# Regrouping one attention group's vector work in a two-layer attention and MLP kernel: heads gathered by DMA, layernorm statistics on ScalarE, two products and a softmax moved behind an output projection, V computed before Q and K

## The chip, the cores and the metric

The kernel runs on one core of a Trainium2 chip. The metric is the device time of one execution in microseconds (us). Before the change it is 1232.96 us, the median of 3 runs (1232.81 to 1233.49). Names of engines: PE is TensorE (PEld its weight loads), DVE is VectorE, ACT is ScalarE, POOL is GpSimd, SP is SyncE. The profiled span is about 2 us shorter than the device time, because it begins at the first instruction and ends at the last.

## The reference

Two layers, each a local dilated attention block and an MLP, with a layernorm ahead of each and a residual after each. The sequence has 2048 rows of 1024; 32 heads of 32; each position attends to 8 positions, two apart.

```python
def _A_ref(x, wqkv, wo):                      # H = 32, Dh = 32, W = 8, dil = 2
    qkv = (x @ wqkv).reshape(B, S, 3, H, Dh)  # -> q, k, v
    idx = pos[:, None] - off[None, :]         # off = arange(8) * 2, masked where negative
    kg, vg = k[:, :, idx_c, :], v[:, :, idx_c, :]
    logits = einsum("bhsd,bhswd->bhsw", q, kg) * scale
    attn = softmax(where(mask, logits, -1e9))
    o = einsum("bhsw,bhswd->bhsd", attn, vg)
    return o.reshape(B, S, D) @ wo
def _B_ref(x, w1, b1, w2, b2):                # F = 3584
    return gelu(x @ w1 + b1) @ w2 + b2
# ... cut: setup
x = x + _A_ref(_layernorm(x), A_wqkv, A_wo)
x = x + _B_ref(_layernorm(x), B_w1, B_b1, B_w2, B_b2)
# ... the same two lines again, same weights
```

## The kernel before

The rows are cut into 4 groups of 512 for each layer; groups are numbered n = 0 to 7 over both layers. PE works through the stages QKV(n), WO(n) (output projection), FFN1(n), FFN2(n) in an order fixed by the program. While PE is in one stage, DVE computes the attention of a later group: eight products q*k for the logits, with a tree of adds (`new_prod`), the softmax (`attend`), the spread of its weights over partitions (`spread`, by DMA), and eight weighted sums of values (`av`). A list of "sides" says after which step of the PE stage each piece is recorded: `at(5, attend, 1)` records the softmax of group 1 after step 5, and `each(av, 1, 10, 2, 0, 4)` records the weighted sums 0 to 3 of group 1 from step 10 on, two steps apart. A scheduler then turns this into one fixed order for each engine, when the program is built; the engine keeps to that order. `hold` forbids that later DVE pieces move ahead of earlier ones.

There are six PSUM accumulators (`acc`); a matmul into a new one waits until an older one has been read out (evicted), and in the FFN2 stage DVE evicts. And qT and kT have one buffer each at this point, so Q of group 3 can't be written before the products of group 2 have read theirs.

```python
def acc_tile():
    return psum.tile([P, T], F32, name="acc", bufs=6)

def head_sum(n, last=True):                  # sum over the 4 partitions of a head, on PE
    # ... cut: L, prod
    for wh in range(2):
        for tb in range(NTT):
            mm(L[tb * H:(tb + 1) * H, wh * 4:(wh + 1) * 4, :], lhsT=smat[:],
               rhs=prod[:, tb, wh * 4:(wh + 1) * 4, :], start=start,
               stop=last, skip_group_check=True, tile_position=(0, tb * H))

def gather(n):                               # the same sum prepared by DMA, added on DVE
    prod = s["prods"].pop(0)
    Lq = bigp.tile([P, HP, W, P], BF16, name="big")
    for j in range(HP):
        pool.dma_start(Lq[:, j, :, :], prod[j::HP, :, :, :])

def attend(n):
    if "Lq" in s:
        # e = Lq[0] + Lq[1], then + Lq[2], + Lq[3]   (DVE)
    else:
        head_sum(n)
    # ... cut: mask, maximum, subtract
    act.on = 1 < n < N - 1                   # the exponential keeps its place in ACT's order
    act.activation(e[:], e[:], ACT.Exp, scale=SCALE)
    # ... cut: sum, reciprocal, multiply -> a

# FFN2, after the last quarter of the contraction, for each of the four row tiles:
    vec.tensor_tensor(out=tmp[:], in0=ps, in1=b2bc[:, out_cols], op=ALU.add)   # the eviction
    vec.tensor_tensor(out=xs, in0=tmp[:], in1=xs, op=ALU.add)

# the stages around the change:
    stage(gen_ffn1(0), sides=at(5, attend, 1) + at(5, spread, 1) + at(5, hold) + each(new_prod, 2, 2, 1)
          + at(10, gather, 2) + at(10, hold) + each(av, 1, 10, 2, 0, 4))
    stage(gen_ffn2(0), sides=at(0, ln_stats_ahead, 3) + at(15, hold) + at(15, ln_a, 3, None, True)
          + each(av, 1, 16, 1, 4, 8) + at(23, hold))
    for n in range(1, N - 2):
        stage(gen_wo(n), sides=at(0, spread, n + 1) if n > 1 else at(7, hold) + at(7, attend, 2))
        stage(gen_qkv(n + 2), sides=(at(0, spread, 2) if n == 1 else []) + each(av, n + 1, 0, 2, 0, 3))
        # ... cut
        gather(n + 2)
        stage(gen_ffn1(n), sides=... + each(av, n + 1, 8, 2, 3, 8))
        if n + 3 < N:
            stage(gen_ffn2(n), sides=at(0, hold) + at(0, attend, n + 2) + at(2, ln_a, n + 3))
```

## Time and profile before

The page's line of busy times (engine, busy us, share of the span, count of instructions) and its chain that ended last (shares of the span by engine and line, where L118 is the helper that issues all matmuls), kernel before:

```profile
PE 1222.2 (99%) x5739; PEld 632.6 (51%) x5789; DVE 861.9 (70%) x922; ACT 307.3 (25%) x491; POOL 87.2 (7%) x207
PE acc L118 98%; DMA wt<-in_A_wqkv_dram 1%; SPq L93 0%; PE L L118 0%; PE L L219 0%; DVE x L93 0%
```

The view of waits of PE alone (who waited for whom: total us, times, longest), kernel before:

```profile
PE acc L219 <- DVE xn L93: 1.5, 1, 1.5
PE acc L118 <- DVE big L93: 1.1, 1, 1.1
PE acc L118 <- DMA wt<-in_A_wqkv_dram: 0.3, 1, 0.3
```

All three waits lie in the first 12.1 us. After that PE never waits. The Trainium skill, "Perfetto Trace Analysis", warns at its top that matmul busy time misjudges the distance to the roofline, because matmuls are pipelined. Here the busy share isn't used for that; what counts is that no other engine ever makes PE wait, so only fewer PE cycles can help, and any new wait costs time.

The cost of one head sum is read from the chain in order of time (start us, duration us, what), kernel before:

```profile
149.78 10.14 PE acc L118 x47
159.93 0.55 PE L L118 x8
160.47 38.31 PE acc L118 x177
```

The eight matmuls of group 1 hold PE for 0.55 us.

Now DVE around FFN2(1), from its timeline (start us, us, engine, line, operation, output<-inputs, count, and in brackets the idle time before it with what ended it), kernel before:

```profile
265.15 1.22 DVE L93 TENSOR_TENSOR e<-big 128x1024 f32<-128x1024 bf16 x1
...
276.26 0.69 DVE L93 TENSOR_TENSOR tmp<-e 128x512 f32<-128x512 f32 x1 [2.47 <-ACT e L93]
...
285.79 4.50 DVE L93 TENSOR_TENSOR big<-abc,vT 128x4096 bf16<-128x4096 bf16 x2 [5.81 <-DMA abc<-a]
...
296.55 2.28 DVE L93 TENSOR_TENSOR big<-qT,kT 128x4096 bf16<-128x4096 bf16 x1
...
371.65 0.69 DVE L93 TENSOR_TENSOR tmp<-acc,b2bc 128x512 f32<-128x512 f32 x1
```

The softmax of group 2 begins at 265.2 (`e<-big`, the first add of its gathered logits; `tmp<-e` at 276.3 is the first step after its exponential). Values of group 2 (`big<-abc,vT`) begin at 285.8, products of group 3 (`big<-qT,kT`) at 296.6, and the first eviction of FFN2(1) (`tmp<-acc,b2bc`) starts at 371.65. PE has no wait there: its timeline shows FFN2(1) as one piece.

```profile
350.35 48.51 PE L118 MATMUL acc<-wt,hT 128*128 128x512 bf16 x219
```

| kernel before | us | view |
|---|---|---|
| device time | 1232.96 | times |
| PE waits after 12.1 us | 0 | waits of PE |
| one head sum on PE | 0.55 | chain in order of time |
| one product or its add | 2.3 | groups (2286 ns; 2291 ns for an add) |
| first eviction of FFN2(1) starts | 371.65 | timeline of DVE |
| FFN2(1) starts / WO(2) starts on PE | 350.35 / 398.70 | timeline of PE |

### The profile page before, as it was taken

What the parts mean: (1) busy time and instruction counts of PE and PEld (TensorE: products, weight loads), DVE (VectorE), ACT (ScalarE), POOL (GpSimd) and SP (SyncE); (2) the same over time, 40 slices, a digit from 0 to 9 for tenths busy, and PEclk for the clock granted to TensorE, in tenths of its full rate; (3) what the DMA queues carried; (4) which work ended last, traced back from release to release, by engine and by line L of the source; (5) the groups of instructions that cost most, each with busy time, mean ns of one, the idle gap of its engine ahead of it and who ended that gap; (6) DMA issues with size and microseconds to landing.
All of it is one profiled execution on the core that took longest, in us unless ns stands there. A gap on an engine that the chain in (4) does not pass through costs nothing.

```text
span 1230.8 us, 13962 instructions
## 1 busy us (share of the span) xinstructions
PE 1222.2 (99%) x5739; PEld 632.6 (51%) x5789; DVE 861.9 (70%) x922; ACT 307.3 (25%) x491; POOL 87.2 (7%) x207
## 2 busy tenths in 40 slices
PE   9999999999999999999999999999999999999998
PEld 7666544456444564445544465444654444444444
DVE  7989899988998599375993759937599797011001
ACT  4343152014320143202431024310244101400310
POOL 3010010010010000100011000010000002000000
PEclk9999999999999999999999999999999999999999
DMA  9954665656556654856447565486664558446441
GB/s 290 300 179 143 182 222 185 201 154 209 181 165 215 180 162 163 229 172 186 150 163 238 171 171 170 158 223 202 171 196 145 188 196 208 151 158 196 155 135 52
DMA packets 219391, 225.06 MB, mean 183 GB/s; under 512 B 68194, under 2 KB 187136, under 8 KB 217024
## 3 DMA queue, kind: packets, MB, share of 16 engines
q1 hardware_dynamic: 214704, 208.69, 55.5%
q0 software_dynamic: 4624, 15.49, 3.3%
q8 instruction: 45, 0.74, 0.2%
q14 instruction: 18, 0.15, 0.0%
HBM read 191.11 MB, written 4.72 MB: 159 GB/s over the span
## 4 chain that ended last, share of the span: by engine, by line
PE 99%; DMA 1%; issue 0%; SPq 0%; DVE 0%
PE acc L118 98%; DMA wt<-in_A_wqkv_dram 1%; SPq L93 0%; PE L L118 0%; PE L L219 0%; DVE x L93 0%
## 5 line engine op out<-in xcount | busy, mean ns | idle before, releaser
L118 PE MATMUL acc<-xnT,wt 128*128 128x512 bf16 (+1 forms) x3392 | 720.9, 375 | 0.4 <-DMA wt<-in_A_wqkv_dram 0.3
L118 PEld LDWEIGHTS <-wt 128*128 128x128 bf16 x3392 | 400.5, 119 | 319.1 <-issue 1.4
L118 PE MATMUL acc<-wt,hT 128*128 128x512 bf16 (+1 forms) x1780 | 386.0, 376 | 2.1
L118 PEld LDWEIGHTS <-hT 128*128 128x128 bf16 x1820 | 178.1, 98 | 208.9
L93 DVE TENSOR_TENSOR big<-big 128x1024 bf16<-128x1024 bf16 (+2 forms) x184 | 245.2, 1360 | 2.2
L93 ACT ACTIVATE hT<-acc,b1T 128x512 bf16<-128x512 f32 x224 | 152.7, 688 | 332.3 <-PE acc L118 332.1
L93 DVE TENSOR_TENSOR big<-qT,kT 128x4096 bf16<-128x4096 bf16 x64 | 143.8, 2286 | 48.4 <-ACT kT L93 47.8
L93 DVE TENSOR_TENSOR big<-abc,vT 128x4096 bf16<-128x4096 bf16 x64 | 144.7, 2286 | 14.0 <-DMA abc<-a 13.4
L93 DVE TENSOR_TENSOR tmp<-acc,b2bc 128x512 f32<-128x512 f32 x56 | 38.6, 690 | 146.7 <-PE acc L118 143.7
L93 ACT CAST qT<-acc 128x512 bf16<-128x512 f32 (+1 forms) x72 | 38.0, 545 | 351.1 <-PE acc L118 351.1
L118 PE MATMUL acc<-wt,oT 128*128 128x512 bf16 x440 | 97.4, 379 | 0.4
L93 DVE BATCH_NORM_STATS2 stats<-x 128x6 f32<-128x512 bf16 x128 | 85.6, 682 | 4.5 <-DMA x<-in_A_x_dram 3.4
L118 PEld LDWEIGHTS <-oT 128*128 128x128 bf16 x448 | 43.8, 98 | 52.8
L93 DVE TENSOR_TENSOR x<-acc,big 128x512 bf16<-128x512 f32 (+1 forms) x9 | 5.7, 633 | 90.0 <-PE acc L118 90.0
L93 ACT CAST vT<-acc 128x512 bf16<-128x512 f32 x64 | 37.5, 586 | 83.3 <-PE acc L118 83.3
L93 ACT CAST kT<-acc 128x512 bf16<-128x512 f32 x64 | 37.4, 587 | 67.0 <-PE acc L118 67.0
L93 POOL TENSOR_TENSOR rstd<-mv,eps_t 128x1 f32<-128x1 f32 x56 | 14.2, 253 | 515.4 <-DVE mv L93 509.4
L93 DVE TENSOR_TENSOR x<-acc,x 128x512 bf16<-128x512 f32 x64 | 42.9, 671 | 4.8 <-PE acc L118 4.4
L93 DVE TENSOR_SCALAR xn<-x,mv,rstd 128x1024 bf16<-128x1024 bf16 x52 | 28.4, 547 | 20.2 <-POOL rstd L93 20.1
L93 DVE TENSOR_TENSOR x<-tmp,x 128x512 bf16<-128x512 f32 x56 | 38.7, 690 | 1.3
L93 POOL DMA_DIRECT2D big<-big x24 | 13.3, 565 | 256.3 <-DVE big L93 237.6
L93 POOL TENSOR_TENSOR rstd<-rstd,mhalf 128x1 f32<-128x1 f32 x56 | 31.0, 553 | 4.4
(68 smaller groups left out, 228.8 us busy)
## 6 DMA issues: line engine op xcount, KB each, us to landing
wt<-in_B_w_dram SPq DMA_DIRECT2D x56, 1024.0 KB, 5.7
wt<-in_B_w_dram SPq DMA_DIRECT2D x64, 896.0 KB, 4.9
wt<-in_A_wqkv_dram SPq DMA_DIRECT2D x46, 1024.0 KB, 5.6
wt<-in_A_wo_dram SPq DMA_DIRECT2D x16, 1024.0 KB, 5.0
big<-big POOLq DMA_DIRECT2D x24, 256.0 KB, 3.6
abc<-a POOLq DMA_DIRECT2D x24, 256.0 KB, 5.3
x<-in_A_x_dram SPq DMA_DIRECT2D x16, 256.0 KB, 6.2
out_dram<-x SPq DMA_DIRECT2D x31, 128.0 KB, 2.1
```

The costliest lines, as they stand in the source:

```text
L93: inst = f(*args, **kwargs)
L118: return pe(nc.tensor.matmul(*args, **kwargs))
```

## The change

The intent is to take the head sum of group 1 off PE (a DMA gather and three DVE adds replace it). DVE is full in that stretch, so room is made: the fourth layernorm's statistics go to ScalarE, and the last two products and the softmax of group 2 go behind WO(1). As these then still need group 2's Q and K when QKV(3) begins, V of group 3 is computed first. The diff, cut to its core:

```diff
     def ln_stats_ahead(g):
+        junk = lnp.tile([P, D], BF16, name="xn", bufs=3)
         for tt in range(NTT):
-            ln_stats(g * NTT + tt, mv_ahead[:, tt, :], rstd_ahead[:, tt, :])
+            # ... cut: t, mean, var, less
+            act.activation(junk[:], x[t][:], ACT.Identity, scale=-1.0 / D, accum_out=less[:])
+            act.activation(junk[:], x[t][:], ACT.Square, bias=less[:], accum_out=var)
+            pool.tensor_scalar(out=mean, in0=less[:], scalar1=-1.0, scalar2=None, op0=ALU.mult)
+            # ... cut: two POOL operations for rstd
 def gen_qkv(...)
+        if v_first:
+            wv = load_qkv(2)          # then V, before Q and K
 def gather(n)
-        Lq = bigp.tile([P, HP, W, P], BF16, name="big")
+        Lq = attp.tile([P, HP, W, P], BF16, name="abc") if n == 1 else bigp.tile([P, HP, W, P], BF16, name="big")
-    def attend(n):
+    def logits(n):                    # up to the subtraction of the maximum
+    def weights(n):                   # exponential, sum, division
-        if n < 2:                     # max by one reduce; spread through DRAM
+        if n == 0:
         stage(q2, sides=each(new_prod, 1, 0, 1, 5, 8))
+        gather(1)
-    stage(gen_ffn1(0), sides=at(5, attend, 1) + at(5, spread, 1) + at(5, hold) + each(new_prod, 2, 2, 1)
-          + at(10, gather, 2) + at(10, hold) + each(av, 1, 10, 2, 0, 4))
+    stage(gen_ffn1(0), sides=each(new_prod, 2, 2, 1, 0, 3) + at(5, hold) + at(5, attend, 1) + at(5, spread, 1) + at(5, hold) + each(new_prod, 2, 6, 1, 3, 6)
+           + at(10, hold) + each(av, 1, 10, 2, 0, 4))
-        stage(gen_wo(n), sides=at(0, spread, n + 1) if n > 1 else at(7, hold) + at(7, attend, 2))
-        stage(gen_qkv(n + 2), sides=(at(0, spread, 2) if n == 1 else []) + each(av, n + 1, 0, 2, 0, 3))
+        stage(gen_wo(n), sides=at(0, spread, n + 1) if n > 1 else at(7, hold))
+        stage(gen_qkv(n + 2, v_first=n == 1), sides=each(av, n + 1, 0, 2, 0, 3) if n > 1 else
+              each(new_prod, 2, 0, 1, 6, 8) + at(1, gather, 2) + at(6, hold) + at(6, logits, 2) + at(15, weights, 2) + at(15, spread, 2) + each(av, 2, 16, 3, 0, 3))
```

More of the change, by code (lines that the diff above doesn't have):

```diff
@@ L205, in ln_stats_ahead @@
     def ln_stats_ahead(g):
+        junk = lnp.tile([P, D], BF16, name="xn", bufs=3)
         for tt in range(NTT):
-            ln_stats(g * NTT + tt, mv_ahead[:, tt, :], rstd_ahead[:, tt, :])
+            t, mean, var = g * NTT + tt, mv_ahead[:, tt, 0:1], mv_ahead[:, tt, 1:2]
+            less = lnp.tile([P, 1], F32, name="less")
+            act.activation(junk[:], x[t][:], ACT.Identity, scale=-1.0 / D, accum_out=less[:])
+            act.activation(junk[:], x[t][:], ACT.Square, bias=less[:], accum_out=var)
+            pool.tensor_scalar(out=mean, in0=less[:], scalar1=-1.0, scalar2=None, op0=ALU.mult)
+            rstd = rstd_ahead[:, tt, :]
+            pool.tensor_scalar(out=rstd, in0=var, scalar1=1.0 / D, scalar2=EPS, op0=ALU.mult, op1=ALU.add)
+            pool.tensor_tensor(out=rstd, in0=rstd, in1=mhalf[:], op=ALU.pow)
     def ln_norm(t, mv, rstd, xn=None):
@@ L318, in new_prod, with gen_qkv @@
                 vec.tensor_tensor(out=tree[-1][:], in0=tree[-1][:], in1=b[:], op=ALU.add)
-    def gen_qkv(n, parts=1, defer=False, qk_pool=None, v_late=False, qk_next=None):
+    def gen_qkv(n, parts=1, defer=False, qk_pool=None, v_late=False, qk_next=None, v_first=False):
         g = n % NG
@@ L326, in gen_qkv, with values @@
         qk_pool = qk_pool or attp
+        if v_first:
+            wv = load_qkv(2)
         wq = wq_first if n == 0 else load_qkv(0)
-        wk = load_qkv(1)
+        if not v_first:
+            wk = load_qkv(1)
+        def values():
+            vT = attp.tile([P, NCH, HALO + T], BF16, name="vT", bufs=2)
+            s["vT"] = vT
+            act.on = n > 2
+            act.copy(vT[:, :, 0:HALO], (zhalo if g == 0 else vhalo)[:])
+            act.on = False
+            for c in range(NCH):
+                ps = qkv_chunk(wv, c, xnT)
+                act.copy(vT[:, c, HALO:], ps[:])
+                yield
+            if g + 1 < NG:
+                act.copy(vhalo[:], vT[:, :, T:T + HALO])
+        if v_first:
+            yield from values()
+            wk = load_qkv(1)
         if n == 0:
@@ L355, in gen_qkv @@
             yield
-        if n > 0 and not v_late:
+        if n > 0 and not v_late and not v_first:
             wv = load_qkv(2)
@@ L370, in gen_qkv @@
             act.copy(khalo[:], kT[:, :, T:T + HALO])
-        vT = attp.tile([P, NCH, HALO + T], BF16, name="vT", bufs=2)
-        s["vT"] = vT
-        if v_late:
-            wv = load_qkv(2)
-        act.on = n > 2
-        act.copy(vT[:, :, 0:HALO], (zhalo if g == 0 else vhalo)[:])
-        act.on = False
-        for c in range(NCH):
-            ps = qkv_chunk(wv, c, xnT)
-            act.copy(vT[:, c, HALO:], ps[:])
-            yield
-        if g + 1 < NG:
-            act.copy(vhalo[:], vT[:, :, T:T + HALO])
+        if not v_first:
+            if v_late:
+                wv = load_qkv(2)
+            yield from values()
     def gather(n):
@@ L424, in attend @@
         vec.tensor_tensor(out=e[:], in0=L[:], in1=mx.unsqueeze(1).to_broadcast([P, W, P]), op=ALU.subtract)
+        s["e"] = e
+    def weights(n):
+        s = st[n]
+        e = s.pop("e")
         act.on = 1 < n < N - 1
@@ L432, in attend @@
         s["a"] = a
+    def attend(n):
+        logits(n)
+        weights(n)
     def spread(n):
@@ L440, in spread @@
         s["oT"] = attp.tile([P, NCH, T], BF16, name="qT" if n == N - 1 else "oT")
-        if n < 2:
+        if n == 0:
             a_d = dram.tile([H, NTT, W, P], BF16, name="a_d")
```

## The prediction

> **What bounds it now.** TensorE. The page's busy line gives PE 1222.2 of 1230.8 us (99%) against 861.9 for DVE (70%) and 307.3 for ACT. The chain that ended last is 98% matmuls into the accumulators, and the view of PE's waits lists three, 2.9 us together, all before 12.1 us. After that PE never waits: in twelve stretches from 12 to 502 us it is busy for 489.2 of 490.0 us. So only two things can move the time: fewer PE cycles, or a new PE stall.
>
> **PE cycles removed.** The head sum of group 1: eight matmuls of 128x512 on 32 columns. Each is shown as 384 ns, but the chain in order of time gives 0.55 us for the eight (159.93 to 160.47). The Trainium skill, "TensorEngine Tiling (Array Packing)", "Theoretical Speedup", says that a dimension of at most 32 allows tiling up to 4x; the trace agrees, 8 x 216 ns / 0.55 us is 3.1. Gain: 0.55 us. All else is moved or lies off the chain.
>
> **What moves on DVE.**
> - FFN1(0)/FFN2(0), 160 to 247 us, DVE all but full; the last oT chunk of group 1 is ready at 247.07, WO(1) starts at 246.75. Out: two products and two adds (9.1 us), statistics (8 x 0.69 + 4 x 0.20 = 6.3 us). In: three adds of 1.21 us, and a fold for the reduce (about 0.2 more). Net about 11.6 us less, so oT should be ready near 235.5. Since PE does not wait there today, this gains nothing by itself.
> - The statistics become 8 ScalarE passes of 128x1024. A copy of that size took 1.04 us, so about 8.5 us, where ACT is idle from 199 to 262. The skill, "ScalarE: Activation LUTs", "Table sets", has cheap functions in every set, so I expect at most one extra table load (1.28 us here). Harmless.
> - Behind WO(1) the 9.1 us come back. V first keeps Q from waiting for its buffer, but K arrives 14 us later, so group 3's products (34 us) start near 291 or later, not interleaved from 296.5 behind av work that began at 285.8. From 291.4 DVE has queued: softmax end 3.7, products 34.3, av of group 2 35, softmax of group 3 with four layernorms 17. That ends near 381, against 371.65 now.
>
> **The risk.** FFN2(1)'s first-half evictions stand behind that queue. The first is ready near 370 and is done today at 372.4. With six accumulators, the third of the second half needs one back at about 377.6. If evictions really start near 381, PE stalls about 4 us. If the scheduler slips evictions into the wait for the exponential, or the queue is shorter, it is 0. I give the stall about even odds. DVE idles 17 us between 372 and 429, so it does not accumulate.
>
> **Prediction.** 1232.96 - 0.55 + half of a stall of up to 4: 1233.9 us, range 1231.8 to 1238.5. Faster by over 2%: 0.01; within 2%: 0.97; slower by over 2%: 0.02.
>
> **What would show it.** PE busy about 0.5 us lower, with eight head-sum matmuls fewer; no idle DVE run-up before WO(1), oT ready 9 to 13 us earlier; 8 new ACT passes of about 1 us; group 1's weights spread directly, without the DRAM copy. A stall shows as PE waiting on DVE (tmp) at 375 to 382; no stall shows as that line absent and a span near 1230.2.
>
> **What would make it wrong.** ScalarE passes landing in FFN1 and delaying Gelu evictions by more than the accumulators cover; the exponential of group 2 waiting in order on ScalarE for late logits, so that K evictions block PE; the gather of group 1 landing late and pushing all of DVE; a buffer (the shared abc or xn) tying the queues together.

## The result and the profile after

The kernel after takes 1244.05 us (median of 5 runs, 1244.02 to 1245.77), the kernel before 1232.96 (5 runs). The ratio is 1.0094, 95% interval 1.008 to 1.0108. Ratios here are the mean time of one kernel's runs over that of the other's of the same rounds, so not quite the ratio of the medians. It is slower, by about 11 us: within 2%, but outside the predicted range of 1231.8 to 1238.5.

Page of the kernel after, the line of busy times:

```profile
PE 1226.0 (99%) x5781; PEld 632.9 (51%) x5781; DVE 860.3 (69%) x915; ACT 315.4 (25%) x507; POOL 107.1 (9%) x211
```

PE's busy share still says 99%, so this line doesn't show the loss. (Some matmul records can be missing from a trace, so the counts of the two pages don't compare either.) The waits of PE, kernel after:

```profile
PE acc L118 <- DVE tmp L93: 10.5, 1, 10.5
PE acc L227 <- DVE xn L93: 1.2, 1, 1.2
PE acc L118 <- DVE big L93: 1.0, 1, 1.0
PE acc L118 <- DMA wt<-in_A_wqkv_dram: 0.2, 1, 0.2
```

The first line is new: one wait of 10.5 us for `tmp`, which is the eviction. The timeline of PE places it in FFN2(1), which is now in two pieces:

```profile
349.65 27.36 PE L118 MATMUL acc<-wt,hT 128*128 128x512 bf16 x126
387.53 22.64 PE L118 MATMUL acc<-wt,hT 128*128 128x512 bf16 x98 [10.53 <-DVE tmp L93]
```

The timeline of DVE, kernel after, with the rows that answer to those of before:

```profile
280.48 1.23 DVE L93 TENSOR_TENSOR e<-big 128x1024 f32<-128x1024 bf16 x1 [7.95 <-DMA big<-big]
...
290.68 0.69 DVE L93 TENSOR_TENSOR tmp<-e 128x512 f32<-128x512 f32 x1 [2.71 <-ACT e L93]
291.33 2.29 DVE L93 TENSOR_TENSOR big<-qT,kT 128x4096 bf16<-128x4096 bf16 x1
...
301.94 2.29 DVE L93 TENSOR_TENSOR big<-abc,vT 128x4096 bf16<-128x4096 bf16 x1 [5.40 <-DMA abc<-a]
...
386.80 0.68 DVE L93 TENSOR_TENSOR tmp<-acc,b2bc 128x512 f32<-128x512 f32 x1
```

The first eviction starts at 386.80 instead of 371.65. The brackets show where DVE stood idle on the way: 7.95 us for the gather of group 2, 2.71 for the exponential, 5.40 for the spread of the weights.

The loss is larger than the wait, because PE's granted clock falls. Stretches of the kernel after (stretch, its length, busy time of PE, PEld, DVE, ACT, POOL with counts, then the granted clock, the DMA share and GB/s):

```profile
377.00:379.00 2.00, 0.01 (x1) 0.00 (x0) 2.00 (x5) 0.05 (x1) 0.74 (x2) 1.00 1.00 335
379.00:382.00 3.00, 0.00 (x0) 0.00 (x0) 2.62 (x6) 2.29 (x2) 0.74 (x2) 0.67 0.60 118
382.00:387.50 5.50, 0.00 (x0) 0.00 (x0) 4.70 (x9) 0.00 (x0) 1.18 (x3) 0.50 0.49 95
387.50:389.50 2.00, 1.97 (x5) 0.71 (x5) 1.85 (x3) 0.00 (x0) 1.89 (x4) 0.50 0.52 190
389.50:391.50 2.00, 2.00 (x9) 0.84 (x8) 1.76 (x4) 0.00 (x0) 0.00 (x0) 0.81 0.90 334
```

The clock goes to half some 3 us into the wait and is still at half when PE resumes: 5 matmuls in 2 us instead of 9 or 10. The Trainium skill, "TensorE: Matmul & The Clock Gate", "What's actually happening", describes this: half clock after at least one idle window of about 3.4 us, full clock again after at least one busy window of that length, by a window that runs freely. The trace agrees in kind; the times of all runs with a wait stand at the end of the experiments.

The sum closes. On PE the stage FFN2(1) lasts from its first matmul to the first of WO(2): 398.70 - 350.35 = 48.35 us before, 410.01 - 349.65 = 60.36 after. The difference of 12.01 is the wait of 10.53 and 1.48 lost mostly to the lower clock. FFN2(1) begins 0.70 us earlier (of which 0.55 is the head sum that is gone). 12.01 - 0.70 = 11.31, and the spans differ by 1242.1 - 1230.8 = 11.3.

### The profile page after: what moved, and what is told of

The parts are those of the page before. It is cut to its first block, busy times and chain, and to the rows that moved or that the text cites. A ratio compares the mean times of both kernels' runs of the same rounds, so it can differ in the third digit from the quotient of the medians.

```text
span 1242.1 us, 14011 instructions
## 1 busy us (share of the span) xinstructions
PE 1226.0 (99%) x5781; PEld 632.9 (51%) x5781; DVE 860.3 (69%) x915; ACT 315.4 (25%) x507; POOL 107.1 (9%) x211
## 4 chain that ended last, share of the span: by engine, by line
PE 69%; DVE 0%; POOL 0%; issue 0%; POOLq 0%
PE acc L118 69%; POOL rstd L93 0%; DVE tmp L93 0%; DVE a L93 0%; DVE xn L93 0%; DVE z L93 0%; DVE x L93 0%; DVE mv L93 0%; POOLq L93 0%
## 5 line engine op out<-in xcount | busy, mean ns | idle before, releaser
L118 PE MATMUL acc<-wt,hT 128*128 128x512 bf16 (+1 forms) x1820 | 389.6, 377 | 10.5 <-DVE tmp L93 10.5
L93 DVE BATCH_NORM_STATS2 stats<-x 128x6 f32<-128x512 bf16 x120 | 79.8, 681 | 3.8 <-DMA x<-in_A_x_dram 2.9
```

What stands on the lines that cost most here:

```text
L93: inst = f(*args, **kwargs)
L118: return pe(nc.tensor.matmul(*args, **kwargs))
```

## The experiments

Twelve runs were made, one of them a repeat; all results were correct. Each job ran the kernel before on the same chip; its medians were 1232.6, 1232.79 and 1232.57 us in the three jobs. The theories:

- **A, late K**: V first brings K of group 3 about 14 us later, and group 3's products with it.
- **B, deferred work**: the 9.1 us of products moved behind WO(1) lengthen DVE's queue. This is what the prediction said "comes back".
- **D, late softmax**: the softmax of group 2, moved to QKV(3), is late by itself.
- **C, the pair**: late K or late softmax alone leaves DVE other work to fill the wait; both together leave it idle, and that idle time is what arrives at the eviction.

### First job: the parts of the loss

**evict_first.** The whole change, with group 3's softmax and group 4's layernorms recorded after FFN2(1)'s first four evictions.

```diff
-            stage(gen_ffn2(n), sides=at(0, hold) + at(0, attend, n + 2) + at(2, ln_a, n + 3))
+            u = 16 if n == 1 else 0
+            stage(gen_ffn2(n), sides=at(u, hold) + at(u, attend, n + 2) + at(u + 2, ln_a, n + 3))
```

> The whole change, but group 3's softmax and the four layernorms of group 4 issued after the first four evictions of FFN2(1) rather than before them. If the loss is only the order of DVE's queue there, the PE wait and the slow clock behind it vanish and the head sum's 0.55 us is left as a gain: 1232.3 to 1232.6 us. If something else of the change costs time (ScalarE passes, the gather through the shared buffer, POOL), it shows here as time over 1233.

Measured: 1232.11 us (ratio 0.9994, 0.9979 to 1.0009). PE has no wait for `tmp`. The timeline of DVE of this run shows the evictions ahead of the softmax:

```profile
369.17 0.69 DVE L93 TENSOR_TENSOR tmp<-acc,b2bc 128x512 f32<-128x512 f32 x1
...
375.07 1.22 DVE L93 TENSOR_TENSOR e<-big 128x1024 f32<-128x1024 bf16 x1
```

So the whole loss is the order of DVE's queue at this one place, and nothing else of the change costs time that shows: DVE idles up front as in the kernel after (7.83 and 5.35 us at the gather and the spread), but that no longer reaches PE.

**prods_back.** Group 2's last two products back in FFN1(0).

```diff
-... each(new_prod, 2, 6, 1, 3, 6)
+... each(new_prod, 2, 6, 1, 3, 8)
-              each(new_prod, 2, 0, 1, 6, 8) + at(1, gather, 2) + ...
+              at(1, gather, 2) + ...
```

> The change with group 2's last two products computed in FFN1(0) again, V still first and the softmax still late. Theory A, late K: the 9.1 us were done at 262 to 272 us, before DVE fell idle for 8 us, so taking them away shortens nothing behind K: the wait stays at 9 to 11 us, about 1243 to 1244 us. Theory B, deferred work: the wait shrinks by about 9 us to 1 or 2, about 1233 to 1235 us.

Measured: 1244.26 us (1.0094). Its wait of PE for the eviction:

```profile
PE acc L118 <- DVE tmp L93: 10.4, 1, 10.4
```

Taking 9.1 us of work out gained nothing, so theory B doesn't explain the loss of the change as it stands (what the same work costs when K is early is shown below, with sm_late). The timeline of DVE of this run says why:

```profile
290.32 0.69 DVE L93 TENSOR_TENSOR tmp<-e 128x512 f32<-128x512 f32 x1 [10.22 <-ACT e L93]
...
301.46 2.29 DVE L93 TENSOR_TENSOR big<-abc,vT 128x4096 bf16<-128x4096 bf16 x1 [5.28 <-DMA abc<-a]
```

The logits are ready at 280, but the exponential stands behind the eight Q copies in ACT's order, and DVE waits 10.22 us with nothing to do, since K has not come. The work that was taken out is replaced by idle time.

**av_late.** The first three value sums of group 2 recorded after all of group 3's products.

```diff
-... each(av, 2, 16, 3, 0, 3))
+... each(av, 2, 24, 1, 0, 3))
```

> The change with the first three value products of group 2 issued after all of group 3's logit products instead of between them. In the trace DVE stood idle 5.4 us at 296.5 to 301.9 with products ready, because the next instruction in its order waited for the spread weights. If that idle is part of the queue, the first eviction comes 5.4 us earlier and the PE wait falls from 10.5 to about 5.1 us; with some lost clock after it, 1237 to 1239 us. If only the sum of work counts and the idle is made up elsewhere, the wait stays near 10 us (1243 to 1244 us).

Measured: 1239.62 us (1.0053). Its wait of PE, and from its timeline of DVE the first eviction:

```profile
PE acc L118 <- DVE tmp L93: 5.2, 1, 5.2
```

```profile
381.40 0.68 DVE L93 TENSOR_TENSOR tmp<-acc,b2bc 128x512 f32<-128x512 f32 x1
```

PE waits 5.22 us. The new order took 10.53 - 5.22 = 5.31 us off the wait, about the 5.40 us of idle in front of the spread. (It is a net figure: this order has a new idle of 1.49 us at 344.61, for a gather, which it makes up elsewhere.) The time is a little above the expected range, because the lower clock took 2.85 us here rather than about 1.5.

**q_first.** The change with Q, K, V in the old order.

```diff
-        stage(gen_qkv(n + 2, v_first=n == 1), ...
+        stage(gen_qkv(n + 2, v_first=False), ...
```

> The change with Q, K, V in the old order for group 3, all else kept (two products and the softmax of group 2 still behind WO(1)). Theory A, late K: the 10.5 us wait for the first eviction of FFN2(1) comes from K arriving 14 us later, which starts group 3's products late; with K back, DVE has products to do from about 277 us, in the wait for group 2's gather, and the first eviction should be done near 375 us, before PE needs the accumulator at 377. No PE wait, about 1232.4 us. Theory B, deferred work: the 9.1 us of products pushed behind WO(1) lengthen the queue; they are still there, so most of the wait (over 7 us) stays, 1240 us or more. If Q waits for the buffer of group 2's Q, PE would also wait near 270 us.

Measured: 1241.24 us (1.007). Theory A's expectation missed; theory B's was met in time (1240 us or more) and just missed in the wait (6.4 us, not over 7). Its waits of PE:

```profile
PE acc L118 <- DVE tmp L93: 6.4, 1, 6.4
...
PE acc L118 <- ACT vT L93: 0.4, 1, 0.4
```

The wait shrank by 4 us, not by 10. Its timeline of DVE:

```profile
280.91 1.23 DVE L93 TENSOR_TENSOR e<-big 128x1024 f32<-128x1024 bf16 x1 [8.23 <-DMA big<-big]
...
331.09 4.49 DVE L93 TENSOR_TENSOR big<-abc,vT 128x4096 bf16<-128x4096 bf16 x2 [7.35 <-DMA abc<-a]
...
383.41 0.68 DVE L93 TENSOR_TENSOR tmp<-acc,b2bc 128x512 f32<-128x512 f32 x1
```

I had expected products of group 3 in the wait for the gather, as K's first copies were done at 276.3 and 278.1. They were not there: in the order that the build fixed, the first softmax add comes ahead of them, and DVE waits for it. At the end all products are done before the spread lands, and DVE idles again. (The short wait for V is a side effect: ScalarE stood 7.11 us at the exponential, in order, and V's copies came late.) So late K alone is not the cause; idle time in a fixed order is part of it, and it can arise in more than one place.

### Second job: which of the two delays

The remaining question is a square with two sides, K early or late and softmax early or late. All four cells have group 2's products in FFN1(0). The cell "both late" is prods_back (10.4 us of wait). "Softmax late" stands for the whole block that the change moved: gather, softmax, spread and the places of the first value sums. vfirst_only and sm_late each differ from prods_back by one side alone; "both early" is built from the kernel before, whose lists for FFN1(0) are cut up differently.

**gather_stats**: both early; the kernel before with only the gather of group 1 and the ScalarE statistics.

```diff
# the kernel before, plus
+        Lq = attp.tile(..., name="abc") if n == 1 else ...     # and gather(1), n == 0 in attend and spread
+        # ln_stats_ahead on ScalarE, as in the change
```

> The kernel before with only the gather of group 1 and the ScalarE statistics; nothing moved behind WO(1), Q first, softmax of group 2 early. Cell 'K early, softmax early'. DVE has 2.5 us less to do before WO(1) (3.8 in, 6.3 out), so oT of group 1 is ready near 244.5 us; FFN2(1)'s first eviction stays near 371. No PE wait; the head sum's 0.55 us is the gain: 1232.2 to 1232.6 us, about what the evictions-first run gave.

Measured: 1232.49 us (0.9999, 0.9986 to 1.0011); no wait for `tmp`; the first eviction at 371.94. The last oT came at 247.46 (246.71 + 0.75), not near 244.5, and still in time.

**vfirst_only**: K late, softmax early.

```diff
# prods_back, with
-... each(new_prod, 2, 6, 1, 3, 8)
+... each(new_prod, 2, 6, 1, 3, 8) + at(10, gather, 2)
-... at(7, hold))
+... at(7, hold) + at(7, attend, 2))
-              at(1, gather, 2) + at(6, hold) + at(6, logits, 2) + at(15, weights, 2) + at(15, spread, 2) + each(av, 2, 16, 3, 0, 3))
+              at(0, spread, 2) + each(av, 2, 0, 2, 0, 3))
```

> Cell 'K late, softmax early' (products of group 2 in FFN1(0), as in the run that put them back). Theory C, idle between two late inputs: late K alone is harmless, since the value products of group 2 can run from 286 us and fill the wait for K; first eviction near 372, no PE wait, about 1232.4 us. Theory A, late K alone: the wait stays near 10 us, 1243 us.

Measured: 1232.44 us (0.9998, 0.9984 to 1.0011); no wait for `tmp`. From its timeline of DVE:

```profile
286.75 4.50 DVE L93 TENSOR_TENSOR big<-abc,vT 128x4096 bf16<-128x4096 bf16 x2 [7.03 <-DMA abc<-a]
...
372.60 0.69 DVE L93 TENSOR_TENSOR tmp<-acc,b2bc 128x512 f32<-128x512 f32 x1
```

The values run from 286.75 on, as in the kernel before, while K is still on its way. PE has a wait of 0.63 us for oT in WO(1) here, which uses up the head sum's 0.55 us: FFN2(1) begins at 350.32.

**sm_late**: K early, softmax late; prods_back with `v_first=False`.

```diff
# prods_back, with
-        stage(gen_qkv(n + 2, v_first=n == 1), ...
+        stage(gen_qkv(n + 2, v_first=False), ...
```

> Cell 'K early, softmax late' (products of group 2 in FFN1(0)). Theory C: group 3's products fill the wait for the late softmax; DVE's queue from 276.5 us on is about 90 us of work, first eviction near 367 to 373, no PE wait, about 1232.4 us; a few us of idle at the spread may cost some of the 5 us of room. Theory D, late softmax alone: wait of 8 us or more, over 1241 us. With the cell 'both late' at 10.4 us measured, C says that only the pair costs.

Measured: 1231.51 us (0.999, 0.9977 to 1.0004); no wait for `tmp`; the first eviction at 375.35, 3.7 us later than before (367 to 373 was expected) and still before PE needs it. Its timeline of DVE:

```profile
279.70 6.69 DVE L93 TENSOR_TENSOR big<-qT,kT 128x4096 bf16<-128x4096 bf16 x3
...
323.03 4.50 DVE L93 TENSOR_TENSOR big<-abc,vT 128x4096 bf16<-128x4096 bf16 x2 [6.70 <-DMA abc<-a]
...
375.35 0.68 DVE L93 TENSOR_TENSOR tmp<-acc,b2bc 128x512 f32<-128x512 f32 x1
```

From 279.70 on group 3's products run where prods_back waits 10.22 us for the exponential. The square reads: both early 0, K late 0, softmax late 0, both late 10.4 us of wait. Theories A and D fall, C holds: either delay alone is filled with other work or stays within the room, the pair is not.

Theory B needs one more look, because q_first and sm_late differ only in the two products of group 2. With the products behind WO(1) (q_first) PE waits 6.40 us and the first eviction starts at 383.41; with them in FFN1(0) (sm_late) it waits 0, and the eviction starts at 375.35. So the moved work does cost when K is early. With K late it costs nothing more (10.53 against 10.40 us), since the exponential runs at 289.6 us (after) or 289.2 (prods_back) either way. What the runs show is that the late softmax costs together with late K or together with the moved work; alone it stays within the room.

**before_plus12**: no part of the change, only delay. Twelve idempotent operations in group 3's softmax.

```diff
+            for _ in range(extra):           # extra = 12 for group 3, else 0
+                vec.tensor_tensor(out=e[:], in0=e[:], in1=e[:], op=ALU.max)
```

> The kernel before with 12 idempotent maximum operations (e = max(e, e), 1.21 us each, about 14.7 us) put into group 3's softmax, ahead of FFN2(1)'s first eviction; no part of the change. If a late first eviction is all that it takes, the eviction ends near 387, PE waits 9 to 10 us from 377.6 on and runs about 2 us at a lower clock: 1243 to 1245 us, like the change itself. If DVE's lateness is not what costs the time, it stays under 1236 us.

Measured: 1246.87 us (1.0112). The expectation was met in kind, and passed in size: the eviction started at 388.47 and ended near 389.2, about 2 us later than expected, PE waited 11.67 us and lost 3.00 more to the clock. A late eviction by itself does what the change does.

### Third job: the threshold, and the parts alone

**before_plus4**: the same with `extra = 4`.

> The kernel before with 4 idempotent maximum operations (4.9 us) instead of 12. The first eviction of FFN2(1) should start near 376.5 us and end just before 377.5, where PE needs the accumulator: a wait of 0 to 1.5 us and no lower clock, 1232.7 to 1234.3 us. A wait of 4 us or more would show that the room is not the 5 us read from the trace.

Measured: 1233.05 us (1.0004, 0.9991 to 1.0018). Its waits of PE and its first eviction:

```profile
PE acc L118 <- DVE tmp L93: 0.3, 1, 0.3
```

```profile
377.06 0.68 DVE L93 TENSOR_TENSOR tmp<-acc,b2bc 128x512 f32<-128x512 f32 x1
```

An eviction that starts at 377.06 costs 0.28 us, so 376.78 would have cost nothing. The kernel before starts it at 371.65, so its room is about 5 us.

**gather_only**: the kernel before with only the gather of group 1 (the edit of gather_stats without the statistics).

> The kernel before with only the gather of group 1. DVE gets about 3.8 us more to do before WO(1), where with gather and ScalarE statistics together the last oT was ready at 246.7 us and PE did not wait. With the statistics (6.3 us) still on DVE oT should be ready at 250 to 253 us and PE, which needs the last chunk near 248, should wait 2 to 5 us in WO(1): 1234 to 1238 us. If PE does not wait, 1232.4 us, and the ScalarE statistics were not needed for the gather.

Measured: 1238.03 us (1.0044, 1.0028 to 1.0059). The waits of PE beyond the start:

```profile
PE acc L118 <- DVE tmp L93: 3.2, 1, 3.2
...
PE acc L118 <- DVE oT L93: 0.3, 1, 0.3
```

The total is at the edge of what I expected and the place was wrong: 3.19 us are lost at the first eviction of FFN2(0), where 3.8 us more of DVE work push it to 227.93, and only 0.27 in WO(1), where I had expected the wait. FFN2(0) lasts 53.39 us (251.50 - 198.11) instead of 48.35: the wait, and 1.85 us of lower clock. So the gather does need room on DVE, and it is the eviction that needs it first.

**stats_only**: the kernel before with only the ScalarE statistics.

> The kernel before with only the ScalarE statistics. DVE has 6.3 us less to do, ScalarE about 9 us more in its gaps, POOL four short operations more. PE does not wait there in either kernel, so no gain: 1232.5 to 1233.1 us, the head sum still on PE. Over 1233.5 us would mean that the ScalarE passes cost PE something.

Measured: 1232.42 us (0.9998, 0.9984 to 1.0011). As expected (0.1 us below the range): it costs PE nothing and gains nothing alone.

**sm_late_again**: the kernel of sm_late, five rounds.

> The same kernel as the one with the late softmax, Q first and products in FFN1(0), again with more rounds, to see whether it beats the kernel before: 1231.4 to 1232.4 us against 1232.8, a gain of the head sum's 0.55 us and no more, below the 2% line.

Measured: 1231.28 us (median of 5, 1231.18 to 1231.71) against 1232.57 (9 runs, 1232.09 to 1233.54); ratio 0.999, 0.9977 to 1.0002. All nine runs of it lie below every run of the kernel before in the same job: at most 1232.10 against at least 1232.63, and at most 1231.71 against at least 1232.09. The gain is 1.3 us, 0.1%, a little more than expected and far below the 2% line, and the interval given for the ratio still includes 1. It is the fastest kernel of this study. Only about 0.55 us of it is explained, by the head sum. Another 0.53 us lies in the start: the remaining head sum, of group 0, begins at 63.66 us in both profiles of this kernel and at 64.19 in that of the kernel before. Other kernels had starts from 63.69 to 64.55, so this may be chance in the first loads; only two of the nine runs were profiled, so whether the others started early is not known.

### All runs at FFN2(1)

"Stage" is the time on PE from the first matmul of FFN2(1) to the first of WO(2); "rest" is stage - 48.35 - wait. Times are medians.

| kernel | first eviction starts | PE waits | stage | rest | time |
|---|---|---|---|---|---|
| evict_first | 369.17 | 0 | 48.34 | 0 | 1232.11 |
| stats_only | 371.11 | 0 | 48.35 | 0 | 1232.42 |
| before | 371.65 | 0 | 48.35 | 0 | 1232.96 |
| gather_stats | 371.94 | 0 | 48.35 | 0 | 1232.49 |
| vfirst_only | 372.60 | 0 | 48.35 | 0 | 1232.44 |
| sm_late_again | 375.25 | 0 | 48.35 | 0 | 1231.28 |
| sm_late | 375.35 | 0 | 48.35 | 0 | 1231.51 |
| before_plus4 | 377.06 | 0.28 | 48.79 | 0.16 | 1233.05 |
| gather_only (delayed in FFN2(0)) | 377.17 | 0 | 48.34 | 0 | 1238.03 |
| av_late | 381.40 | 5.22 | 56.42 | 2.85 | 1239.62 |
| q_first | 383.41 | 6.40 | 57.17 | 2.42 | 1241.24 |
| prods_back | 386.31 | 10.40 | 60.67 | 1.92 | 1244.26 |
| after | 386.80 | 10.53 | 60.36 | 1.48 | 1244.05 |
| before_plus12 | 388.47 | 11.67 | 63.02 | 3.00 | 1246.87 |

Whatever made the eviction late, each microsecond of lateness beyond a fixed point is a microsecond of PE wait. The point is 26.62 us after the first matmul of FFN2(1): in all six runs with a wait, the start of the eviction less the wait less the start of the stage gives 26.62 (after: 386.80 - 10.53 - 349.65). In gather_only the stage began at 355.54, so 377.17 was early enough.

The rest is lost mostly to the clock, and its size follows from when the clock came back. The table gives the times read in steps of 0.1 us (`prof <label> --windows`, the column of the granted clock), in us; durations are worked out before rounding, and the last line is the wait of gather_only in FFN2(0):

| kernel | PE idle from | clock halves | PE resumes | clock full again | half clock lasts |
|---|---|---|---|---|---|
| av_late | 376.92 | 380.79 | 382.14 | 387.62 | 6.83 |
| q_first | 377.75 | 381.94 | 384.15 | 388.76 | 6.83 |
| prods_back | 376.65 | 380.42 | 387.04 | 390.66 | 10.24 |
| after | 377.01 | 380.01 | 387.53 | 390.26 | 10.24 |
| before_plus12 | 377.54 | 381.34 | 389.21 | 394.99 | 13.65 |
| gather_only | 225.47 | 229.12 | 228.66 | 232.53 | 3.41 |

In every one of the six the half clock lasts 1, 2, 3 or 4 times 3.41 us: within a run, the two changes of the clock lie a whole number of such steps apart, whatever the wait. Half of the time between PE's return and the full clock is 2.74, 2.31, 1.81, 1.36 and 2.89 us in the first five lines, 0.11 or 0.12 us less than their rest; a remainder of this kind also stands in before_plus4 (0.16), where the clock stayed at 1.00. So the loss depends on where PE's return falls between two steps, and not on the length of the wait.

## Why the prediction was wrong

- **"PE never waits ... only two things can move the time: fewer PE cycles, or a new PE stall."** Right. The result is made of just these: 0.55 us less and one new wait, with the slow clock behind it.
- **Head sum 0.55 us.** Right: the eight matmuls at 159.9 us are gone, and FFN2(1) begins 0.70 us earlier.
- **Where the stall would be.** Right in place and mechanism: the first eviction of FFN2(1) stands behind the softmax of group 3 and four layernorms, and PE waits for an accumulator from 377.0 us (predicted "about 377.6"). evict_first shows it, since it moves nothing else.
- **"That ends near 381 ... PE stalls about 4 us."** This is the step that failed. The term is the DVE queue from 291 us. I summed its work (3.7 + 34.3 + 35 + 17 us, worked out from the durations of before) and took DVE to be busy throughout. The work was right (from 291.33 to 386.80 DVE took 95.47 us, less 5.40 of idle 90.07, against a sum of 90); the queue also held 5.40 us of idle, in front of the first value sum that waited for the spread weights while products of group 3 were ready behind it. The trace of before already had an idle of this kind, 5.81 us for the same spread. The eviction came at 386.8, and the wait was 10.53 us rather than 4. av_late, which removes this idle, waits 5.22 us. The other 1.2 us are mostly that its queue ends at 381.40 rather than 381, and that PE needs the accumulator at 376.9 rather than 377.6: with the head sum gone FFN2(1) begins earlier (by 0.70 us in the kernel after), and the deadline moves with it.
- **A stall costs its length.** Not stated but used, and wrong: the lower clock after it added 1.48 us here and up to 3.00 in other runs. This term was missing from the sum.
- **"I give the stall about even odds", and half of it in the estimate.** The chances that evictions slip in between, or that the queue is shorter, were not worked out. Half of a mis-sized 4 put the estimate where neither outcome was.
- **"Behind WO(1) the 9.1 us come back."** They do run there (products at 261.9 to 266.4 us, their adds from 267.6 to 272.2), but they are not why the eviction is late: prods_back takes them out again and still waits 10.40 us. The cause is that K and the softmax are late together, as the square of four cells shows. (With K early they would have cost 6.40 us of wait, as q_first shows beside sm_late.)
- **"oT should be ready near 235.5."** Mis-sized and harmless: it was ready at 242.44 (241.69 + 0.75) against 247.07 before. DVE stood idle for 5.50 us before FFN2(0)'s first eviction at 217.54, since the second half of group 1's value sums is recorded behind a hold.
- **ScalarE passes.** About as predicted in cost: eight passes of about 1.05 and 1.14 us, plus 0.19 us each to read the accumulator, and no extra table load (17 in both kernels; the skill, "ScalarE: Activation LUTs", "Table sets: the hidden batching unit", names identity among the cheap functions that are in every set, and this trace agrees for Identity beside Gelu and shows the same for Square). They did not wait for the idle stretch that I named: the scheduler put half of them at 141 to 147 us and half among the Gelu evictions at 188 to 194 us. The twelve short POOL operations that go with them took 0.49 to 2.63 us each, where the additions and powers of that size for the other layernorms mostly take 0.19 and 0.55; why was not tested. stats_only shows that all this costs nothing.
- **The spread without the DRAM copy.** Right: four DMA issues into the DRAM tile are left, instead of eight.

Still open: where sm_late's gain beyond the head sum's 0.55 us comes from, and what share of a step PE must be busy for the clock to come back at its end.

## What to carry to other kernels

When an in-order engine is costed as a queue, add up its work and also its waits: for each late input ask what stands next in the fixed order, not what would be ready. Two delays that are each harmless, because other work fills the gap, can cost in full when they fall together and leave nothing to fill it. Work that frees a resource of the bound engine (here the eviction of an accumulator) belongs ahead of work that only a later stage needs; recording it first took away the whole loss.

## What the Trainium skill lacked or had wrong

- "TensorE: Matmul & The Clock Gate", "What's actually happening" gives a window of 3413 ns that runs freely, which fits the multiples of 3.41 us above, and says that the moment of change therefore varies by 500 ns either way, while a note below it has one kernel start with 6, 11 or 14 slow matmuls. Here the full clock came back 2.7 us (after), 3.6 (prods_back), 4.6 (q_first), 5.5 (av_late) and 5.8 (before_plus12) after PE had resumed, a spread of 3.1 us, which fits the note and not the 500 ns. The lost time was 1.5 to 3.0 us for waits of 5 to 12 us.
- The same section doesn't say how much of a window must be busy or idle. Worked out from the table above: a step in which PE was busy for 35% (q_first), 60% (av_late) or 69% (before_plus12) did not bring the full clock back at its end, and one of 80% (after) did; a step in which PE was idle for 88% (after) or 87% (gather_only) was enough to halve it. So the wait of 3.19 us in gather_only, shorter than the window, halved the clock, half a microsecond after PE had resumed; the table at the page's "Why this matters for your kernels" does warn of gaps of over about 3 us. (Ends of matmuls are modelled in the profile, so the shares are estimates.)
- No page says what a fixed instruction order does to an estimate by sums: here 5.40 us of idle with ready work behind it, which is half of the wait of 10.53.
